# A slot of its own for the diagonal that spreads the maxima, and a generator step between PE products and VectorE's reads

## Chip, cores and metric

The kernel runs on one core of a Trainium2 chip. The metric is the device time of one execution in microseconds (us). A core has five engines that matter here, each with its own instruction queue: PE (TensorE, the matrix products), DVE (VectorE), ACT (ScalarE), POOL (GpSimd) and SP (SyncE, which here issues the DMAs). An engine works its queue in the order of the program and stands still while the instruction at its head waits for another engine or a DMA.

## What is computed

Three stages, each fed by the one before. The reference, cut to what matters:

```python
# 1: attention over a window of 128 positions, 4 x 8 heads of 64, 576 positions
x = attention(q, k, v)                    # 2304 x 512
# 2: soft mixture: 8 experts of 4 slots each
logits = x @ phi
d = softmax(logits, over tokens); slots = d.T @ x
slot_out[e] = relu(slots[e] @ w1[e]) @ w2[e]
x = softmax(logits, over slots) @ slot_out
# 3: mixture over all tokens, gated by Sinkhorn
P = exp(x @ w_gate - max)
for _ in range(8):
    P /= P.sum(1) + 1e-9;  P /= P.sum(0) + 1e-9;  P *= N / E
out = sum over e of P[:, e] * (relu(x @ m1[e]) @ m2[e])
```

The third stage takes most of the time: eight experts of 512 x 1024 and 1024 x 512 weights over 2304 tokens. Here these weights are called `m1` and `m2`.

## The kernel before

The third stage runs a loop over 72 pairs of token tiles, nine pairs for each expert `e`. A pair `m` has seven steps `k_` = 0 to 6. Each product in L1045 is a block of twelve fp16 matmuls (a high and a low half of either factor); the seven products of a pair are those of Strassen's scheme in Winograd's form. Ahead of them, in the first two steps, `emit_z` (L973) makes the hidden values of the next pair in PSUM tiles `z`. From `z`, `left(m+1, k_)` makes the operands `ops` and the sums `s` of the next pair: ACT the high halves and relus, DVE the sums (L998) and some low halves (L986), POOL the other low halves (L1005). The products accumulate in PSUM tiles `x` and `y`; DVE adds them into `acc` (L1057 for expert 0, L1059 for the others) between the products of one `x` tile, so a product that goes on in `x` has to wait until the add in front of it has read the tile.

Beside this loop runs a generator `side`. The call `next(side, None)` in L1194 takes it one step further in each of the 63 steps of an expert, and each `yield` in it ends such a step. What a step issues stands, on every engine, behind the products of that step and ahead of its `left`. In step 4 of an expert's last pair the rest is flushed (L1200). `side` prepares the next expert:

- `prep_w1(e)`: sixteen fp32 products of `st` and `m1` on PE (L682, 32 instructions, since an fp32 matmul is issued twice), the largest magnitude of each row on DVE (`am`, L686), then `spread` (L553): the identity times that column gives a diagonal `dg`; `largest` (L557) multiplies it by a matrix of ones, so that every partition gets all the maxima; DVE takes their maximum (`ar`, L696), makes a power of two of it (L90 to L92), and ACT and DVE write the scaled high and low halves `sh` and `sl` (L701, L702). Two steps later sixteen DMAs copy these to `stk` (L710), eight from each.
- `magnitude(e)`: eight steps of absolute sums of `m2` on ACT (L565), then a maximum (L569).
- `prep_w2a(e)`: `spread` and `largest` again for the maxima of `m2`, then the scaled and differenced halves of `m2` on ACT and POOL in 44 steps.

For expert 0 the first pairs also hold `gate` (products of `st4` with the gate's weights, L904 and L911, a maximum L916, `spread`, `largest`, an exponential into `prob`) beside `magnitude(1)`, and then the eight Sinkhorn rounds (L929 to L942, on DVE with one product on PE, L936) beside `prep_w1(1)` and `prep_w2a(1)`; `par` takes one step of each in turn, and the Sinkhorn side rests in every third.

The diagonal `dg` and the half `sl` are tiles of the pool `mp` with the same tag `sl` and one buffer: each takes its place only when the readers of the one before are done.

Of the kernel before, what the change touches and what calls it, by code (L numbers as in the profile page):

```python
# [8 lines left out]
F32 = mybir.dt.float32  # L9
# [15 lines left out]
def tile_kernel(ctx: ExitStack, tc: tile.TileContext, q, k, v, phi, w1, w2, w_gate, m1, m2, rel, out):  # L25
# [40 lines left out]
    def w1_at(nm, e, dc, f0, n):  # L66
        return wt[nm, e][:, dc * F + f0:dc * F + f0 + n]
# [10 lines left out]
    def warm(pool, tag, w_, n):  # L78

        ps = pool.tile([128, 512], F32, tag=tag, name="warm") if pool is not None else tag  # L80
        for _ in range(n):
            x_ = w_[:, 0:min(256, w_.shape[1])]
            nc.tensor.matmul(ps[:, 0:x_.shape[1]], lhsT=idn, rhs=x_, start=True, stop=True)
        return ps

    def pow2(pool, am, name):

        pw = pool.tile([128, 1], F32, tag=name + "p", name=name + "p")
        iv = pool.tile([128, 1], F32, tag=name + "i", name=name + "i")
        nc.vector.tensor_scalar_max(pw, am, TINY)  # L90
        nc.vector.tensor_single_scalar(pw.bitcast(I32), pw.bitcast(I32), 0x7F800000, op=ALU.bitwise_and)  # L91
        nc.vector.reciprocal(iv, pw)  # L92
        return pw, iv

    with tc.manual_schedule():
        with ExitStack() as ab:
# [5 lines left out]
            with ExitStack() as at:  # L102
# [4 lines left out]
                sp = at.enter_context(tc.tile_pool(name="sp", bufs=2))  # L107
# [426 lines left out]
            mp = ab.enter_context(tc.tile_pool(name="mp", bufs=2, reuse_waits="tile", side="right"))  # L534
# [11 lines left out]
            w2c = {}  # L546
            wsum = {}
            bound = {}

            def spread(am):  # L550

                dg = mp.tile([128, 128], F32, tag="sl", name="dg", bufs=1)
                nc.vector.tensor_scalar_mul(dg, idn, am)  # L553
                return dg

            def largest(dg, ps):
                nc.tensor.matmul(ps, lhsT=ones, rhs=dg, start=True, stop=True)  # L557
# [14 lines left out]
            def prep_w2a(e, place):  # L572
                if e not in bound:
                    yield from magnitude(e)
                dg = spread(bound.pop(e))
                yield
                ps = place()
# [100 lines left out]
            def prep_w1(e, pool=None, tag=None):  # L678
                ps = pool.tile([128, 512], F32, tag=tag, name="m") if pool is not None else pmt
                for dc in range(DC):  # L680
                    for kk in range(4):
                        nc.tensor.matmul(ps[32 * kk:32 * kk + 32, 0:256], lhsT=st[:, dc, :],  # L682
                                         rhs=w1_at("m1", e, dc, 256 * kk, 256),
                                         start=(dc == 0), stop=(dc == DC - 1), tile_position=(0, 32 * kk))
                am = mp.tile([128, 1], F32, tag="am1", name="am1")
                nc.vector.tensor_reduce(out=am, in_=ps[:, 0:256], axis=AX.X, op=ALU.max, apply_absolute_value=True)  # L686
                dg = spread(am)
                if e:
                    yield
                largest(dg, ps[:, 256:384])  # L690
                if e == 0:
                    warm(pool, tag, wt["m1", e], 2)
                else:
                    yield
                ar = mp.tile([128, 1], F32, tag="ar1", name="ar1")
                nc.vector.tensor_reduce(out=ar, in_=ps[:, 256:384], axis=AX.X, op=ALU.max)  # L696
                pw, iv = pow2(mp, ar, "w1")
                nc.vector.tensor_copy(out=inv_s[:, e:e + 1], in_=pw)
                sh = mp.tile([128, 256], F16, tag="sh", name="sh", bufs=1)
                sl = mp.tile([128, 256], F16, tag="sl", name="sl", bufs=1)  # L700
                nc.scalar.activation(out=sh, in_=ps[:, 0:256], func=AF.Copy, scale=iv)  # L701
                nc.vector.scalar_tensor_tensor(out=sl, in0=ps[:, 0:256], scalar=iv, in1=sh,  # L702
                                               op0=ALU.mult, op1=ALU.subtract)
                yield
                yield
                stk[e] = mp.tile([128, F], F16, tag="stk", name="stk")
                if e:
                    for i, part in enumerate((sh, sh, sl, sl)):
                        for kk in range(4):
                            nc.sync.dma_start(out=stk[e][32 * i:32 * i + 32, 256 * kk:256 * kk + 256],  # L710
                                              in_=part[32 * kk:32 * kk + 32, :])
                    yield
                    return
                pss = [pool.tile([128, 512], F32, tag=tag, name="m") for _ in range(4)]
                for lhs, rhs in ((selh, sh), (sell, sl)):
                    for kk in range(4):
                        rows = slice(32 * kk, 32 * kk + 32)
                        nc.tensor.matmul(pss[kk][:, 0:256], lhsT=lhs[rows], rhs=rhs[rows], start=lhs is selh,
                                         stop=lhs is sell, tile_position=(32 * kk, 0))
                for kk in range(4):  # L720
                    (nc.vector.tensor_copy if kk % 2 else nc.scalar.copy)(
                        out=stk[e][:, 256 * kk:256 * kk + 256], in_=pss[kk][:, 0:256])
                yield

            with ExitStack() as bs:
# [154 lines left out]
                for _ in prep_w1(0, pb, "b"):  # L880
                    pass
# [3 lines left out]
            with ExitStack() as ms:  # L885
                ap_ = ms.enter_context(tc.tile_pool(name="acc", bufs=1, reuse_waits="tile"))
                acc = ap_.tile([128, NT, DM], F32, name="acc")

                pmt = pm.tile([128, 512], F32, name="m")
                sp = ms.enter_context(tc.tile_pool(name="sums", bufs=1, reuse_waits="tile"))  # L890
                pz = ms.enter_context(tc.tile_pool(name="pz", bufs=2, reuse_waits="tile", space=PSUM))
                px = ms.enter_context(tc.tile_pool(name="px", bufs=2, reuse_waits="tile", space=PSUM))
                py = ms.enter_context(tc.tile_pool(name="py", bufs=1, reuse_waits="tile", space=PSUM))
# [1 line left out]
                def gate():  # L895

                    st4 = sp.tile([128, DC, 4, NS], F32, name="st4")
                    sgb = sp.tile([128, 4, E], F32, name="sgb")
                    nc.gpsimd.memset(sgb, 0.0)
                    nc.vector.tensor_copy(out=st4, in_=st.unsqueeze(2).to_broadcast([128, DC, 4, NS]))  # L900
                    yield
                    ps = pmt
                    for dc in range(DC):
                        nc.tensor.matmul(ps[:, 0:E], lhsT=st4[:, dc].rearrange("p a b -> p (a b)"),  # L904
                                         rhs=wg_sb[:, dc, :], start=(dc == 0), stop=(dc == DC - 1))
                    for i in range(4):
                        nc.scalar.copy(out=sgb[32 * i:32 * i + 32, i, :], in_=ps[32 * i:32 * i + 32, 0:E])
                    yield
                    yield
                    for g in range(NG):  # L910
                        nc.tensor.matmul(ps[:, 32 * g:32 * g + 32], lhsT=cTf[:, g, :],  # L911
                                         rhs=sgb.rearrange("p a b -> p (a b)"), start=True, stop=True)
                    l2 = ps[:, 0:NT * E]
                    mx = mp.tile([128, 1], F32, tag="mx", name="mx")
                    mg = mp.tile([128, 1], F32, tag="mg", name="mg")
                    nc.vector.tensor_reduce(out=mx, in_=l2, axis=AX.X, op=ALU.max)  # L916
                    dg = spread(mx)
                    yield
                    largest(dg, ps[:, 256:384])
                    yield  # L920
                    nc.vector.tensor_reduce(out=mg, in_=ps[:, 256:384], axis=AX.X, op=ALU.max, negate=True)
                    nc.scalar.activation(out=prob.rearrange("p a b -> p (a b)"), in_=l2, func=AF.Exp, bias=mg)
                    yield
# [237 lines left out]
                for m in range(NM):  # L1161
                    e, n = divmod(m, NP)
# [77 lines left out]
```

## Time and profile before

| | us |
|---|---|
| median of 3 runs | 984.17 (983.91 to 984.69) |
| profiled execution | 984.86 |
| its span on the core | 983.1 |
| PE busy in the span | 950.5 |
| DVE busy | 744.9 |
| ACT busy | 624.4 |
| POOL busy | 574.3 |

The loop over the pairs begins 211 us into the span; attention and the second stage lie before it. An expert takes some 93.5 us. Times in the rows are counted from the start of the span. In the timeline a row is one instruction or some alike, with its start, its length, engine, line, operation, tiles and shapes; a bracket at the end tells how long the engine stood idle before it and which instruction or DMA ended that.

### The profile page before, as it was taken

The numbers are of one execution on the slowest core, as the hardware profiler recorded it, in microseconds if no ns is written. First come the engines' busy times: TensorE is split into PE (matmuls) and PEld (weight loads), VectorE is DVE, ScalarE is ACT, GpSimd is POOL, SyncE is SP. The second block draws the span as 40 slices with busy tenths as digits, with TensorE's granted clock in tenths as the row PEclk, the third lists the DMA queues.
The fourth block names the chain that finished last, engine by engine and source line by source line (L and its number), as shares of the span: only waits on it lengthen the run. The fifth ranks groups of instructions, "written<-read, shape, count | busy, mean of one in ns | idle before, by whom it ended". The sixth has DMA issues, their size and how long they took to land.

```text
span 983.1 us, 24146 instructions
## 1 busy us (share of the span) xinstructions
PE 950.5 (97%) x9341; PEld 814.4 (83%) x9341; DVE 744.9 (76%) x1924; ACT 624.4 (64%) x1529; POOL 574.3 (58%) x685
## 2 busy tenths in 40 slices
PE   8999999889799999999999999999999999999997
PEld 7887886447588888888888888888888888888886
DVE  6988896675697687777777777877777777777775
ACT  5877884746467678766666665766476656664542
POOL 2222210204488568947884797499658956995442
PEclk9999999999899999999999999999999999999999
DMA  8999997970200220031005001300220020001222
GB/s 174 257 226 219 254 281 284 368 267 2 96 1 2 94 90 1 2 109 76 1 2 182 2 1 54 131 2 2 89 95 2 1 94 5 2 2 28 60 44 65
DMA packets 94497, 90.07 MB, mean 92 GB/s; under 512 B 63664, under 2 KB 67632, under 8 KB 94384
## 3 DMA queue, kind: packets, MB, share of 16 engines
q1 hardware_dynamic: 94384, 88.54, 30.9%
q8 instruction: 73, 1.20, 0.5%
q14 instruction: 40, 0.33, 0.1%
HBM read 81.97 MB, written 4.72 MB: 88 GB/s over the span
## 4 chain that ended last, share of the span: by engine, by line
PE 67%; DVE 2%; ACT 0%; issue 0%
PE x L1045 34%; PE y L1045 26%; PE z L973 6%; PE m L682 1%; DVE acc L1059 1%; DVE ops L986 0%; DVE sl L702 0%; ACT sh L701 0%; PE m L557 0%; DVE ar L696 0%; DVE w1i L92 0%; DVE w1p L91 0%; DVE w1p L90 0%; DVE acc L1057 0%; PE m L936 0%
## 5 line engine op out<-in xcount | busy, mean ns | idle before, releaser
L1045 PEld LDWEIGHTS <-ops 128*128 128x128 f16 x6048 | 593.4, 98 | 77.2 <-issue 5.5
L1005 POOL TENSOR_TENSOR ops<-s,ops 128x512 f16<-128x512 f32 x287 | 331.9, 1159 | 234.4 <-ACT ops L1002 196.6
L1045 PE MATMUL x<-w2h,ops 128*128 128x256 f16 x2304 | 415.5, 273 | 4.0 <-DVE acc L1059 3.1
L1045 PE MATMUL y<-w2h,ops 128*128 128x256 f16 x1728 | 319.5, 273 | 0.3 <-POOL ops L1005 0.2
L1002 ACT CAST ops<-s 128x512 f16<-128x512 f32 x288 | 177.8, 618 | 218.5 <-DVE s L998 216.0
L1045 PE MATMUL x<-w2l,ops 128*128 128x256 f16 x1152 | 314.8, 274 | 0.0
L1045 PE MATMUL y<-w2l,ops 128*128 128x256 f16 x864 | 235.6, 273 | 0.0
L1059 DVE SCALAR_TENSOR_TENSOR acc<-x,pe,acc 128x256 f32<-128x256 f32 x252 | 121.8, 483 | 71.1 <-PE x L1045 70.0
L983 ACT ACTIVATE ops<-z 128x512 f16<-128x512 f32 x216 | 128.6, 596 | 36.9 <-PE z L973 34.0
L986 DVE SCALAR_TENSOR_TENSOR ops<-z,ops 128x512 f16<-128x512 f32 x216 | 147.0, 681 | 0.0
L1059 DVE SCALAR_TENSOR_TENSOR acc<-y,pe,acc 128x256 f32<-128x256 f32 x189 | 91.4, 484 | 61.4 <-PE y L1045 60.5
L640 POOL TENSOR_TENSOR w2l<-w,w2h 128x256 f16<-128x256 f32 x168 | 112.9, 676 | 0.0
L998 DVE SCALAR_TENSOR_TENSOR s<-z,r 128x512 f32<-128x512 f32 x144 | 98.2, 682 | 10.3 <-ACT r L994 7.1
L998 DVE SCALAR_TENSOR_TENSOR s<-z,s 128x512 f32<-128x512 f32 x144 | 98.1, 681 | 1.4 <-POOL t L640 0.7
L181 POOL TENSOR_SCALAR qn<-qn 128x128 f32<-128x128 f32 x64 | 33.8, 536 | 100.5 <-DMA qn<-in_q_dram 70.7
L973 PE MATMUL z<-ct,stk 128*128 128x256 f16 x576 | 86.8, 274 | 3.2 <-DVE ops L986 2.5
L643 ACT CAST w2h<-w 128x256 f16<-128x256 f32 x168 | 67.0, 402 | 2.3 <-POOL w L640 2.3
L973 PEld LDWEIGHTS <-stk 128*128 128x128 f16 x576 | 55.6, 98 | 13.1 <-DVE ops L986 3.3
L230 ACT ACTIVATE et<-et,mx 128x192 f32<-128x192 f32 (+2 forms) x144 | 61.3, 434 | 1.2 <-DVE mx L221 1.1
L202 PE MATMUL s<-kT,qT 128*128 128x192 f32 (+2 forms) x288 | 50.2, 317 | 0.1
L221 DVE CUSTOM_DVE_ANT_0 et<-s,rel_sb 128x192 f32<-128x192 f32 (+2 forms) x144 | 40.1, 326 | 8.5 <-PE s L202 8.0
L202 PEld LDWEIGHTS s<-kT,qT 128*128 128x128 f32 x288 | 43.7, 191 | 3.4 <-issue 3.4
(196 smaller groups left out, 949.6 us busy)
## 6 DMA issues: line engine op xcount, KB each, us to landing
w<-in_moe_w_dram SPq DMA_DIRECT2D x68, 512.0 KB, 6.4
w<-in_moe_w_dram SPq DMA_DIRECT2D x14, 2048.0 KB, 8.3
kn<-in_k_dram SPq DMA_DIRECT2D x36, 128.0 KB, 5.4
qn<-in_q_dram SPq DMA_DIRECT2D x36, 128.0 KB, 4.9
v<-in_v_dram SPq DMA_DIRECT2D x18, 256.0 KB, 5.1
out_dram<-acc SPq DMA_DIRECT2D x34, 128.0 KB, 2.4
w<-in_moe_w_dram SPq DMA_DIRECT2D x2, 1024.0 KB, 8.4
stk<-sh SPq DMA_DIRECT2D x56, 16.0 KB, 1.8
```

Source lines behind the costliest of these rows:

```text
L202: nc.tensor.matmul(ps[gg][:, j, col:192], lhsT=qT[:, g, j, :], rhs=kT[:, g, j, k0:k1], start=True, stop=True)
L230: nc.scalar.activation(out=runs[hh], in_=runs[hh], func=AF.Exp, bias=mx[:, hh:hh + 1], scale=-1.0, accum_out=sm[:, hh:hh + 1])
L640: nc.gpsimd.tensor_tensor(out=out_, in0=x_, in1=y_, op=ALU.subtract)
L643: nc.scalar.copy(out=hi[:, i, r], in_=src[:, r])
L973: nc.tensor.matmul(ps[:, i], lhsT=stk[e][:, 128 * ft:128 * ft + 128], rhs=ct.rearrange("p (a n) t -> p a n t", a=2)[:, :, n, :], start=Tru ...
L983: nc.scalar.activation(out=ops_[m][:, k_, 0], in_=zb(m, i, j), func=AF.Relu)
L986: nc.vector.scalar_tensor_tensor(out=ops_[m][:, k_, 1], in0=zb(m, i, j), scalar=0.0, in1=ops_[m][:, k_, 0], op0=ALU.max, op1=ALU.subtract)
L998: nc.vector.scalar_tensor_tensor(out=new_sum(m, nm), in0=zb(m, i, j), scalar=0.0, in1=o, op0=ALU.max, op1=op)
L1002: nc.scalar.copy(out=ops_[m][:, k_, 0], in_=sm_[m, nm])
L1005: eng.tensor_tensor(out=ops_[m][:, k_, 1], in0=sm_[m, nm], in1=ops_[m][:, k_, 0], op=ALU.subtract)
L1045: nc.tensor.matmul(out_, lhsT=a_[:, k_, l_, i, :], rhs=r_[:, k_, i, :], start=(first and j == 0), stop=(j == 11), skip_group_check=True)
L1059: nc.vector.scalar_tensor_tensor(out=o, in0=ps, scalar=pe_[e][:, t:t + 1], in1=o, op0=ALU.mult, op1=ALU.add)
```

## The change

`spread` takes its tile from a pool and tag in `dgp`. At first that is the old slot; when the third stage begins, it becomes a tag `dg` of its own in the pool `sums`, which is opened some lines earlier than before. A `yield` is put between the sixteen products of `prep_w1` and the reduce that reads them (for experts 1 and on), and one between the last products of `gate` and its reduce.

```diff
--- before.py
+++ after.py
@@ -546,10 +546,12 @@
             w2c = {}
             wsum = {}
             bound = {}
+            dgp = [mp, "sl"]
 
             def spread(am):
 
-                dg = mp.tile([128, 128], F32, tag="sl", name="dg", bufs=1)
+                pool, tag = dgp
+                dg = pool.tile([128, 128], F32, tag=tag, name="dg", bufs=1)
                 nc.vector.tensor_scalar_mul(dg, idn, am)
                 return dg
 
@@ -683,6 +685,8 @@
                                          rhs=w1_at("m1", e, dc, 256 * kk, 256),
                                          start=(dc == 0), stop=(dc == DC - 1), tile_position=(0, 32 * kk))
                 am = mp.tile([128, 1], F32, tag="am1", name="am1")
+                if e:
+                    yield
                 nc.vector.tensor_reduce(out=am, in_=ps[:, 0:256], axis=AX.X, op=ALU.max, apply_absolute_value=True)
                 dg = spread(am)
                 if e:
@@ -885,9 +889,10 @@
             with ExitStack() as ms:
                 ap_ = ms.enter_context(tc.tile_pool(name="acc", bufs=1, reuse_waits="tile"))
                 acc = ap_.tile([128, NT, DM], F32, name="acc")
+                sp = ms.enter_context(tc.tile_pool(name="sums", bufs=1, reuse_waits="tile"))
+                dgp[:] = [sp, "dg"]
 
                 pmt = pm.tile([128, 512], F32, name="m")
-                sp = ms.enter_context(tc.tile_pool(name="sums", bufs=1, reuse_waits="tile"))
                 pz = ms.enter_context(tc.tile_pool(name="pz", bufs=2, reuse_waits="tile", space=PSUM))
                 px = ms.enter_context(tc.tile_pool(name="px", bufs=2, reuse_waits="tile", space=PSUM))
                 py = ms.enter_context(tc.tile_pool(name="py", bufs=1, reuse_waits="tile", space=PSUM))
@@ -910,6 +915,7 @@
                     for g in range(NG):
                         nc.tensor.matmul(ps[:, 32 * g:32 * g + 32], lhsT=cTf[:, g, :],
                                          rhs=sgb.rearrange("p a b -> p (a b)"), start=True, stop=True)
+                    yield
                     l2 = ps[:, 0:NT * E]
                     mx = mp.tile([128, 1], F32, tag="mx", name="mx")
                     mg = mp.tile([128, 1], F32, tag="mg", name="mg")
```

The lines after the edits are numbered some higher in the changed kernel: L553 is L555 there, L557 is L559, L686 is L690, L696 is L700, L702 is L706, L929 to L942 are L935 to L948, L986 is L992, L998 is L1004, L1057 is L1063 and L1059 is L1065.

The first place is on DVE, in the Sinkhorn rounds: the end of the row half of a round and what follows, with the waits of each instruction. `am_3647` are the maxima of expert 1's `m2`; In the waits DMAHW stands for DMAs, the other names are engines. Before:

```order
L932 TENSOR_TENSOR prob<-prob,rs 128x144 [waits DVE_49]
L934 TENSOR_REDUCE c_3963<-prob 128x8 [waits DVE_49]
L553 TENSOR_SCALAR dg<-idn,am_3647 128x128 [waits DMAHW4_49,DMAHW5_49,DMAHW3_49,DMAHW6_49,DMAHW2_49,DMAHW7_49,DMAHW1_49,DMAHW0_49]
L998 SCALAR_TENSOR_TENSOR s_4007<-z,r_3983 128x512 [waits PE_49,Activation_49,Pool_49]
L1057 TENSOR_TENSOR acc<-y,acc 128x256 [waits PE_49]
L986 SCALAR_TENSOR_TENSOR ops<-z,ops 128x512
L939 TENSOR_SCALAR c_4042<-m 128x8 [waits PE_49]
L941 RECIPROCAL c_4042<-c_4042 128x8 [waits DVE_49]
L942 TENSOR_TENSOR prob<-prob,c_4042 128x144 [waits DVE_49]
```

and now:

```order
L938 TENSOR_TENSOR prob<-prob,rs 128x144 [waits DVE_49]
L940 TENSOR_REDUCE c_3963<-prob 128x8 [waits DVE_49]
L1004 SCALAR_TENSOR_TENSOR s_4003<-z,r_3966 128x512 [waits PE_49,Activation_49,Pool_49]
L1063 TENSOR_TENSOR acc<-y,acc 128x256 [waits PE_49]
L555 TENSOR_SCALAR dg<-idn,am_3647 128x128
L992 SCALAR_TENSOR_TENSOR ops<-z,ops 128x512
L945 TENSOR_SCALAR c_4041<-m 128x8 [waits PE_49]
L947 RECIPROCAL c_4041<-c_4041 128x8 [waits DVE_49]
L948 TENSOR_TENSOR prob<-prob,c_4041 128x144 [waits DVE_49]
```

The diagonal has moved behind a sum and an add, and it has no wait for DMAs any more; the reduce `ar` that reads the result has moved behind a second sum and add.

The second place is on DVE too, in the first pair of expert 2, where the weights `m1` of expert 3 are prepared. Before, from the reduce `am` on:

```order
L686 TENSOR_REDUCE am_6405<-m 128x1
L553 TENSOR_SCALAR dg<-idn,am_6405 128x128
L1059 SCALAR_TENSOR_TENSOR acc<-x,pe,acc 128x256
L998 SCALAR_TENSOR_TENSOR s_6431<-z,r_6410 128x512
L1059 SCALAR_TENSOR_TENSOR acc<-y,pe,acc 128x256
L696 TENSOR_REDUCE ar_6447<-m 128x1
L90 TENSOR_SCALAR w1p<-ar_6447 128x1
L91 TENSOR_SCALAR w1p<-w1p 128x1
L92 RECIPROCAL w1i<-w1p 128x1
L698 COPY inv_s<-w1p 128x1
L702 SCALAR_TENSOR_TENSOR sl<-m,w1i,sh 128x256
L986 SCALAR_TENSOR_TENSOR ops<-z,ops 128x512
```

and now the same stretch, one add earlier:

```order
L1065 SCALAR_TENSOR_TENSOR acc<-x,pe,acc 128x256
L690 TENSOR_REDUCE am_6405<-m 128x1
L555 TENSOR_SCALAR dg<-idn,am_6405 128x128
L1004 SCALAR_TENSOR_TENSOR s_6430<-z,r_6407 128x512
L1065 SCALAR_TENSOR_TENSOR acc<-y,pe,acc 128x256
L992 SCALAR_TENSOR_TENSOR ops<-z,ops 128x512
L1065 SCALAR_TENSOR_TENSOR acc<-x,pe,acc 128x256
L700 TENSOR_REDUCE ar_6464<-m 128x1
L90 TENSOR_SCALAR w1p<-ar_6464 128x1
L91 TENSOR_SCALAR w1p<-w1p 128x1
L92 RECIPROCAL w1i<-w1p 128x1
L702 COPY inv_s<-w1p 128x1
```

The add of `x` has moved ahead of the reduce, and the low half `ops` and the next add of `x` have moved ahead of the chain from `ar` to `sl`. On PE the matmul L557 stands one block of products later than before, at this place and at each like it; the order of the DMAs on SP is unchanged.

## Rows read from the trace of the kernel before

**Rows 1.** Page, part 1: busy time of the engines, share of the span, instructions.

```profile
PE 950.5 (97%) x9341; PEld 814.4 (83%) x9341; DVE 744.9 (76%) x1924; ACT 624.4 (64%) x1529; POOL 574.3 (58%) x685
```

**Rows 2.** Stretches: length, busy PE, PEld, DVE, ACT, POOL; granted clock, DMA share, GB/s.

```profile
400.00:480.00 80.00, 79.48 (x743) 70.22 (x741) 61.06 (x124) 52.59 (x111) 58.11 (x67) 1.00 0.16 57
```

**Rows 3.** Waits of the whole span: us in total, times, the longest.

```profile
DVE am L686 <- PE m L682: 18.9, 8, 2.6
...
DVE dg L553 <- DMA stk<-sl: 7.0, 1, 7.0
...
PE x L1045 <- DVE acc L1059: 3.1, 6, 0.5
...
PE z L973 <- DVE ops L986: 2.5, 2, 1.6
```

**Rows 4.** Timeline around the diagonal of expert 1's second weights.

```profile
248.57 0.41 DVE L934 TENSOR_REDUCE c<-prob 128x8 f32<-128x144 f32 x1
...
249.73 4.97 SPq L710 DMA_DIRECT2D stk<-sl  x8
...
250.02 0.29 PE L936 MATMUL m<-c,ones 128*128 128x8 f32 x2
...
255.94 0.29 DVE L553 TENSOR_SCALAR dg<-idn,am 128x128 f32<-128x128 f32 x1 [6.96 <-DMA stk<-sl]
...
256.28 0.80 PE L557 MATMUL m<-dg,ones 128*128 128x128 f32 x2 [5.97 <-DVE dg L553]
...
257.20 0.37 PE L1045 MATMUL y<-w2h,ops 128*128 128x256 f16 x1
...
259.72 0.36 PE L1045 MATMUL x<-w2h,ops 128*128 128x256 f16 x1
```

**Rows 5.** Timeline of the first pair of expert 2: PE, DVE, POOL.

```profile
423.54 1.93 PE L682 MATMUL m<-w,st 128*32 128x256 f32 x32
...
425.55 0.42 DVE L686 TENSOR_REDUCE am<-m 128x1 f32<-128x256 f32 x1 [2.56 <-PE m L682]
...
427.17 0.39 PE L557 MATMUL m<-dg,ones 128*128 128x128 f32 x2
...
427.37 0.48 DVE L1059 SCALAR_TENSOR_TENSOR acc<-y,pe,acc 128x256 f32<-128x256 f32 x1
427.39 0.27 PE L1045 MATMUL x<-w2h,ops 128*128 128x256 f16 x1
...
427.77 0.28 DVE L696 TENSOR_REDUCE ar<-m 128x1 f32<-128x128 f32 x1
...
428.70 0.27 PE L1045 MATMUL y<-w2h,ops 128*128 128x256 f16 x1
...
429.57 0.68 DVE L986 SCALAR_TENSOR_TENSOR ops<-z,ops 128x512 f16<-128x512 f32 x1
...
430.17 0.47 DVE L1059 SCALAR_TENSOR_TENSOR acc<-x,pe,acc 128x256 f32<-128x256 f32 x1
...
430.69 0.27 PE L1045 MATMUL x<-w2h,ops 128*128 128x256 f16 x1 [0.52 <-DVE acc L1059]
...
432.02 2.28 POOL L1005 TENSOR_TENSOR ops<-s,ops 128x512 f16<-128x512 f32 x2 [1.15 <-ACT ops L1002]
...
435.28 0.38 PE L1045 MATMUL x<-w2h,ops 128*128 128x256 f16 x2
...
436.37 0.60 PE L973 MATMUL z<-ct,stk 128*128 128x256 f16 x4
```

**Rows 6.** Stretches as in rows 2; then one line's instructions: ns min/median/max, first and last start.

```profile
257.20:259.70 2.50, 2.50 (x12) 1.72 (x12) 2.33 (x10) 1.03 (x3) 1.16 (x1) 0.50 1.01 354
256.00:288.00 32.00, 30.91 (x263) 26.29 (x264) 30.48 (x72) 20.60 (x48) 23.39 (x27) 0.94 0.18 66
...
L932 DVE TENSOR_TENSOR prob<-prob,rs x8: 307/485/966, 237.4 to 297.2; 128x144 f32<-128x144 f32 x8
```

**Rows 7.** Timeline at the end of the Sinkhorn rounds, PE.

```profile
299.68 0.50 PE L973 MATMUL z<-ct,stk 128*128 128x256 f16 x3 [1.65 <-DVE ops L986]
```

## The prediction

> **Bound.** The page was read first. TensorE (PE) is busy 950.5 of 983.1 us [rows 1]. A busy PE need not be at its peak, so the stages were read next: in a steady stretch of 80 us PE is busy 79.48 and VectorE (DVE) only 61.06 [rows 2]. There the products of L1045 follow each other without a break, and a change can win only what PE still waits for. The third view, the waits, names four things that touch the edited lines [rows 3]: DVE's diagonal `dg` waits once, 7.0 us, for the DMAs that read `sl`; DVE's reduce `am` waits eight times for the sixteen products of `prep_w1`, 18.9 us in all; PE waits for DVE's adds before `x` products six times, 3.1 us; PE waits twice for DVE's `ops` before `z`, 2.5 us. The last view, the timeline, says which of these waits reach PE: the first [rows 4] and the third [rows 5]. DVE works strictly in program order, so whatever is queued behind a waiting instruction waits too.
>
> **Part 1** is the slot of its own. Before, `dg` and the half-weights `sl` share one buffer. For expert 1 the diagonal of `prep_w2a` comes right after the DMAs are issued (the magnitudes were taken earlier, beside the gate), so it must wait until all eight transfers out of `sl` have landed. DVE ends its work at 248.98 and starts `dg` at 255.94: 6.96 us. PE has `largest` next in its queue and stands still 5.97 us [rows 4]. Behind the waiting `dg`, DVE holds the sums `s`, the add and the `ops` of the next pair, and ScalarE and GpSimd wait for those in turn. In the changed order the same `dg` carries no DMA wait, as the listing in front shows. For experts 2 to 7 nine steps of `magnitude` lie between the DMAs and `dg`, and `dg` waits for nothing there (the wait stands once in the row), so the slot costs and gains nothing. The diagonal's multiply itself is unchanged; a 512-byte tile per partition is added and no instruction.
>
> What is this wait worth? Two bounds. PE: with `dg` ready, `L936` at 250.02 would be followed by `largest` and then by the `y` products; such an fp32 product takes PE about 0.22 us (L1045 resumed 0.22 us after `largest` started at 427.17 [rows 5]), so `y` would start at 250.46 and the next `x` 1.31 us later, at 251.77. It started at 259.72, so PE lost 7.95 us [rows 4, 5]. DVE: 6.96 us. Between the two I take DVE's, because DVE is last in this stage: from 256 to 288 it is busy 30.48 of 32.00 us, since the Sinkhorn rounds lie on it beside the products' own work [rows 6], and the stage ends with PE waiting 1.65 us for DVE's `ops` at 299.68 [rows 7]. A DVE that starts 6.96 us earlier and has the same work ends 6.96 us earlier. So part 1 gives 7.0 us, ends 6.0 (PE's idle row alone) and 8.0.
>
> The clock speaks to that choice. The twelve `y` products after the stall took 2.52 us instead of 1.31; the granted clock in that stretch was 0.50, the 1.2 GHz level, and PE had stood idle 5.97 us before [rows 4, 6]. The Trainium skill (TensorE: Matmul & The Clock Gate, section HAM oscillation) says that an idle gap throttles the array and that the next matmuls pay for it; by this rule PE gets the slow stretch back too and part 1 is worth 7.95 us. That is PE's bound above, and it counts in full only where DVE keeps up.
>
> **Part 2** is the step between the products and the reduce in `prep_w1`. Once per expert from 2 to 7 (six times; the rows show the preparation of expert 3) PE gets sixteen fp32 products at 423.54, 1.93 us long. DVE is free at 422.99 and stands before the reduce until 425.55, 2.56 us, with the add of `x` behind it [rows 5]. It never catches up before the next add of `x`: that runs at 430.17, and the `x` product needs it. PE's `y` started at 428.70, its twelve take 1.31 us (427.39 to 428.70), so the next product was due at 430.01; it came at 430.69. The loss is 0.68 us (the row's 0.52 counts from the modelled end of the last matmul) [rows 5].
>
> Now the new order, with the starts of these rows (an add takes DVE 0.40 us from start to start, an `ops` or `s` 0.60, the chain from `ar` to `sl` 1.80, that is 427.77 to 429.57). The add of `x` goes in front of the reduce: it needs the `x` products that end just before 423.54 plus their drain, so it runs at 423.65. The reduce then still waits until 425.55; the wait doesn't vanish, only what is behind it shrinks. `s` follows the reduce and the diagonal; the `y` add runs at 427.37 as before, `ops` at 427.77, and the critical add of `x` as soon as its products end, about 428.68 instead of 430.17. PE needs it at about 430.0, `largest` being a step later, so the 0.68 us is gone. What is late next: the chain now lies behind that add, 429.08 to 430.88, and then come `s`, add, `s`, add, `ops`, add, `s`, add, `ops`: 430.88 + 5 x 0.60 + 4 x 0.40 = 435.5. The last `ops` frees the PSUM buffer of the second `z`, which came at 436.37 and without the stall is due at 435.69 [rows 5]. So it just fits, with 0.2 us to spare. The gain is 6 x 0.68 = 4.1 us, ends 0 and 4.1.
>
> **Part 3** is the step in the gate, and what shifts behind both steps. The gate's reduce moves behind one sum and one add. PE does not wait for it: the matrix `prob` is first read by Sinkhorn only after the ten rounds of `magnitude`, so I cost it at nothing; that cover is the magnitudes' ten rounds against the gate's seven, now eight. The reduce of expert 1's preparation (one of the eight in [rows 3]) also sheds a sum and an add from behind it, 0.60 + 0.40 us, but the chain to `sl` then waits for a later `largest`; I take 0, with ends 0 and 0.4, an estimate: the 1.0 us less the 0.60 of one more instruction's wait. Every later step of the preparation moves by one, and so do its DMAs: SyncE's queue keeps its order, and `stk` is needed only by the next expert, tens of us later. At the end of an expert what is left over is flushed at once: one more copy on ScalarE and one more subtract on GpSimd than before. Their results are used seven products later; nothing.
>
> Sum: 7.0 + 4.1 = 11.1 us. The profiled execution took 984.86 us, of which 983.1 is the span; it would take 973.8. The median of the runs shown is 984.17, 0.69 lower, so 973.1 is forecast.
>
> **Rivals.**
> 1. *DVE is late at `z`.* The chain of 1.80 us behind the critical add lands on the second `z`, where I count only 0.2 us to spare; if `sl` waits for ScalarE longer, part 2 gives nothing. Then 984.17 - 7.0 - 0.4, about 976.8. For: the margin is thin. Against: DVE idles again in a steady stretch (61.06 of 80.00).
> 2. *PE keeps all of it.* DVE, freed at the gate, at the reduce and at `dg`, gets far enough ahead that PE's `z` waits vanish as well: 7.95 + 2.5 [rows 3] + 4.1 = 14.6, so 969.6. For: DVE's waits before 250 also shrink. Against: 30.48 of 32.00.
> 3. *The saved time is lost to GpSimd.* The multiply of a Sinkhorn round takes 0.307 us at best, 0.485 in the middle and 0.966 at worst [rows 6], the longer ones while GpSimd is busy with weights (23.39 of 32 us). If the twelve multiplies of the last six rounds all went from the middle to the worst, that is 12 x 0.48 = 5.8 us, of which about half is already paid: 3 us, giving 976. The Trainium skill (SBUF - State Buffer, section Who interferes with whom) speaks for it: a VectorE instruction with two SBUF inputs contends with a GpSimd instruction that reads SBUF, and the change pushes both together. Against: the rounds that ran beside an idle GpSimd before 249 do so still.
> 4. *Slower.* The weights' subtracts on GpSimd shift by one step against the products' low halves (L1005). The tightest of those, for the second sum, ends at 433.18 (the first of the two at 432.02, 1.16 each) and PE reads it at 435.28 [rows 5]: 2.1 us of slack. A subtract takes 0.68, so from four in front of it PE would wait; at 0.68 in each of the some 44 pairs with a preparation that is 30 us, 1003. Against: one step of the preparation issues one subtract.
> 5. *It doesn't do what it says*: the slot still waits, on whatever lay in that memory. 984. Against: the order shows no wait at all.
>
> **Chances.** Forecast 0.57, rival 1 0.14, rival 2 0.15, rival 3 0.07, rival 4 0.03, rival 5 0.04. The forecast's own range is 971.7 to 974.5. With rivals 1, 2 and 3 the range is 969.4 to 977.2; rivals 4 and 5 and the tails stay out. Faster by over 0.2% (2 us, about what a measurement here tells from no change): 0.93; within: 0.04; slower: 0.03.
>
> **What shows it.** In the changed trace `dg` has no DMA releaser, PE's 5.97 us is gone and the clock holds at 1.00 from 250 to 260; the gaps of PE for `z` in the Sinkhorn stage stay (rival 2 if they go). The six waits for the add of `x` are gone and no wait of `z` stands in their place (rival 1 if one does); the period from one expert's sixteen products to the next falls by 0.68 us; DVE's reduce still waits some 1.5 us each. I would be wrong if the Sinkhorn stage gave back the start, or if the first pair of each expert got a new gap.

## The result, and the profile after

The changed kernel takes **975.25 us** (median of four runs, 974.01 to 977.06), the kernel before 984.04 us (four runs, 983.87 to 984.69) on the same chip. The ratio is 0.9911, with a 95% interval of 0.9894 to 0.9928: faster by 8.8 us, where 11.1 were forecast. The profiled execution of the changed kernel took 975.7 us, of which 973.9 is the span. Of the lines named below, L682 is now L684, L710 is L714, L973 is L979, L1005 is L1011 and L1045 is L1051; in the experiments the numbers differ from those of the changed kernel by the one to three lines that each edit leaves out or adds.

Page, part 1, after (engine, busy us, share of the span, instructions; answers to [rows 1]):

```profile
PE 947.7 (97%) x9341; PEld 813.8 (84%) x9341; DVE 744.7 (76%) x1924; ACT 624.8 (64%) x1529; POOL 575.3 (59%) x685
```

The instructions are the same. Of the 9.2 us by which the span shrank, 6.4 are idle time of PE and 2.8 busy time. The waits, after (engine, line, what it waited for: us in total, times, the longest; answers to [rows 3]):

```profile
DVE am L690 <- PE m L684: 10.1, 7, 1.7
...
PE z L979 <- DVE ops L992: 3.8, 2, 2.2
...
DVE am L690 <- PE m L942: 1.8, 1, 1.8
```

Two rows of before have no counterpart: the wait of `dg` for the DMAs out of `sl` (7.0 us) and the six waits of the `x` products for DVE's add (3.1 us). The reduce's waits are shorter, as forecast, and still there. But one of them has a releaser that it did not have before, Sinkhorn's product L942, and the waits at `z` have grown from 2.5 to 3.8 us.

The steady stretch answers to [rows 2] (length, busy PE, PEld, DVE, ACT, POOL; granted clock, DMA share, GB/s): PE now has no gap in it at all.

```profile
400.00:480.00 80.00, 80.00 (x749) 70.83 (x747) 62.26 (x127) 51.96 (x111) 58.09 (x67) 1.00 0.17 57
```

The diagonal of expert 1's second weights, in the timeline of after (answers to [rows 4]; start us, us, engine, line, operation, and in brackets the idle time ahead and its releaser): it runs with no DMA releaser, in front of the transfers that it used to wait for.

```profile
251.55 0.65 DVE L555 TENSOR_SCALAR dg<-idn,am 128x128 f32<-128x128 f32 x1
251.85 4.96 SPq L714 DMA_DIRECT2D stk<-sl  x8
```

Two marks divide the span so that each part of the change can be read alone: the first `z` of expert 0 (at 211.63 before, 211.37 after) and the last waiting `z` of the Sinkhorn rounds ([rows 7] before; 294.61 after, below). From the one to the other runs expert 0's stage with the gate, Sinkhorn and expert 1's preparation; behind the second lie the rest of expert 0 and experts 1 to 7, with the preparations of experts 2 to 7.

| | first `z` to last waiting `z` | from there to the span's end |
|---|---|---|
| before | 299.68 - 211.63 = 88.05 | 983.1 - 299.68 = 683.42 |
| after | 294.61 - 211.37 = 83.24 | 973.9 - 294.61 = 679.29 |

The tail gave 4.13 us, what part 2 was said to give. The stage gave 4.81 us instead of 7.0. So the question is where 2.2 us of the stage went. The timeline of after around expert 1's preparation shows a candidate:

```profile
237.31 1.93 PE L684 MATMUL m<-w,st 128*32 128x256 f32 x32
...
240.50 0.29 PE L942 MATMUL m<-c,ones 128*128 128x8 f32 x2
240.82 0.42 DVE L690 TENSOR_REDUCE am<-m 128x1 f32<-128x256 f32 x1 [1.80 <-PE m L942]
...
242.90 1.16 POOL L1011 TENSOR_TENSOR ops<-s,ops 128x512 f16<-128x512 f32 x1 [2.32 <-ACT ops L1008]
243.11 1.11 DVE L948 TENSOR_TENSOR prob<-prob,c 128x144 f32<-128x144 f32 x1
...
244.15 0.28 DVE L700 TENSOR_REDUCE ar<-m 128x1 f32<-128x128 f32 x1
...
246.87 0.68 DVE L992 SCALAR_TENSOR_TENSOR ops<-z,ops 128x512 f16<-128x512 f32 x1
...
247.61 1.03 PE L979 MATMUL z<-ct,stk 128*128 128x256 f16 x4 [2.22 <-DVE ops L992]
...
294.61 0.61 PE L979 MATMUL z<-ct,stk 128*128 128x256 f16 x4 [1.56 <-DVE ops L992]
```

The sixteen products end at 239.24, but the reduce begins only at 240.82. One step later in the order, it stands behind Sinkhorn's first product, which writes other columns of the same PSUM tile `pmt` (384 on, where the reduce reads 0 to 255), and the program has it wait for that too. (The Trainium skill, PSUM — Partial Sum Buffer, section PSUM bank collisions raise a hardware error, asks for waits by bank and quadrant, not by address; by this rule the wait is needed as long as both lie in one bank. The trace agrees in so far as a wait stands at disjoint columns; no run leaves it out, and none gives Sinkhorn's sums a tile of their own.) Behind the reduce the chain `ar` to `sl` comes late, and with it the `ops` that frees the buffer of `z`. PE stands still 2.22 us, where the same `z` waited 0.81 before:

```profile
246.95 0.61 PE L973 MATMUL z<-ct,stk 128*128 128x256 f16 x4 [0.81 <-DVE ops L986]
```

And the twelve `y` products behind that gap take 2.56 us (248.43 to 250.99) instead of 1.31, at a granted clock of 0.50, the 1.2 GHz level:

```profile
248.40:251.00 2.60, 2.60 (x15) 1.82 (x13) 1.72 (x5) 1.46 (x4) 0.15 (x2) 0.50 0.09 19
```

### The profile page after: what moved, and what is told of

It is laid out like the page before. It is cut to its first block, busy times and chain, and to the rows that moved or that the text cites. A ratio compares the mean times of both kernels' runs of the same rounds, so it can differ in the third digit from the quotient of the medians.

```text
span 973.9 us, 24118 instructions
## 1 busy us (share of the span) xinstructions
PE 947.7 (97%) x9341; PEld 813.8 (84%) x9341; DVE 744.7 (76%) x1924; ACT 624.8 (64%) x1529; POOL 575.3 (59%) x685
## 4 chain that ended last, share of the span: by engine, by line
PE 69%; DVE 0%; issue 0%
PE x L1051 35%; PE y L1051 27%; PE z L979 6%; PE m L684 1%; PE m L559 0%; DVE ops L992 0%; DVE acc L1065 0%; DVE acc L1063 0%; PE m L942 0%
## 5 line engine op out<-in xcount | busy, mean ns | idle before, releaser
L1051 PEld LDWEIGHTS <-ops 128*128 128x128 f16 x6048 | 592.9, 98 | 72.8 <-issue 1.8
L1011 POOL TENSOR_TENSOR ops<-s,ops 128x512 f16<-128x512 f32 x287 | 332.7, 1161 | 228.2 <-ACT ops L1008 227.3
L1051 PE MATMUL x<-w2h,ops 128*128 128x256 f16 x2304 | 414.3, 273 | 1.8 <-ACT ops L989 0.7
L1051 PE MATMUL y<-w2h,ops 128*128 128x256 f16 x1728 | 319.5, 273 | 0.0
L1051 PE MATMUL x<-w2l,ops 128*128 128x256 f16 x1152 | 314.2, 273 | 0.0
L1051 PE MATMUL y<-w2l,ops 128*128 128x256 f16 x864 | 235.6, 273 | 0.0
L1065 DVE SCALAR_TENSOR_TENSOR acc<-x,pe,acc 128x256 f32<-128x256 f32 x252 | 121.7, 483 | 77.4 <-PE x L1051 76.1
L992 DVE SCALAR_TENSOR_TENSOR ops<-z,ops 128x512 f16<-128x512 f32 x216 | 146.9, 680 | 0.0
L1065 DVE SCALAR_TENSOR_TENSOR acc<-y,pe,acc 128x256 f32<-128x256 f32 x189 | 91.3, 483 | 58.4 <-PE y L1051 58.1
L1004 DVE SCALAR_TENSOR_TENSOR s<-z,r 128x512 f32<-128x512 f32 x144 | 98.2, 682 | 11.2 <-ACT r L1000 7.2
L1004 DVE SCALAR_TENSOR_TENSOR s<-z,s 128x512 f32<-128x512 f32 x144 | 98.1, 682 | 5.0 <-ACT ops L989 4.8
L979 PE MATMUL z<-ct,stk 128*128 128x256 f16 x576 | 86.8, 274 | 4.5 <-DVE ops L992 3.8
L979 PEld LDWEIGHTS <-stk 128*128 128x128 f16 x576 | 55.6, 98 | 14.4 <-DVE ops L992 4.8
```

What stands on the lines that cost most here:

```text
L979: nc.tensor.matmul(ps[:, i], lhsT=stk[e][:, 128 * ft:128 * ft + 128], rhs=ct.rearrange("p (a n) t -> p a n t", a=2)[:, :, n, :], start=Tru ...
L992: nc.vector.scalar_tensor_tensor(out=ops_[m][:, k_, 1], in0=zb(m, i, j), scalar=0.0, in1=ops_[m][:, k_, 0], op0=ALU.max, op1=ALU.subtract)
L1004: nc.vector.scalar_tensor_tensor(out=new_sum(m, nm), in0=zb(m, i, j), scalar=0.0, in1=o, op0=ALU.max, op1=op)
L1011: eng.tensor_tensor(out=ops_[m][:, k_, 1], in0=sm_[m, nm], in1=ops_[m][:, k_, 0], op=ALU.subtract)
L1051: nc.tensor.matmul(out_, lhsT=a_[:, k_, l_, i, :], rhs=r_[:, k_, i, :], start=(first and j == 0), stop=(j == 11), skip_group_check=True)
L1065: nc.vector.scalar_tensor_tensor(out=o, in0=ps, scalar=pe_[e][:, t:t + 1], in1=o, op0=ALU.mult, op1=ALU.add)
```

## The experiments

Theory A, then: the slot is worth its 7 us, the step is worth 4.1 us in experts 2 to 7, and for expert 1 the step costs some 2 us, because the reduce then also waits for Sinkhorn's product. Rivals: the slot itself is worth only 4.8 (B); the gate's step is what costs (C); the step is late by itself, whatever Sinkhorn does (D).

**The parts apart.** `slot_only` has neither step:

```diff
-                if e:
-                    yield
                 nc.vector.tensor_reduce(out=am, in_=ps[:, 0:256], ...
...
-                    yield
                     l2 = ps[:, 0:NT * E]
```

> Only the slot of its own; neither the gate nor the preparation gives a step. Theory A (the slot is worth the forecast 7 us; the preparation's step costs about 2 us for expert 1, where the reduce of the maxima then also waits for Sinkhorn's product that writes the same PSUM tile, and it gives 6 x 0.69 = 4.1 us for experts 2 to 7): 984.0 - 7.2 = 976.8 us; the wait of the product z at 247.61 us after is short again (0.8 us before) and the reduce of expert 1 begins within 1 us of its products' end. Theory B (the step costs nothing for expert 1, and the slot itself is worth only the 4.8 us that the stage lost, the rest being given back in Sinkhorn's chain): 984.0 - 4.8 = 979.2 us, with a wait of about 2 us at the same z.

Measured: 977.22 us against 984.46 for the kernel before in the same rounds, 7.24 us faster (in brackets, here and below, the ratio to before with its 95% interval: 0.9922, 0.9909 to 0.9935). The same stretch of its timeline, and the last waiting `z`:

```profile
237.46 1.93 PE L684 MATMUL m<-w,st 128*32 128x256 f32 x32
239.46 0.42 DVE L688 TENSOR_REDUCE am<-m 128x1 f32<-128x256 f32 x1 [1.79 <-PE m L684]
...
241.66 0.28 DVE L698 TENSOR_REDUCE ar<-m 128x1 f32<-128x128 f32 x1
...
246.43 0.61 PE L976 MATMUL z<-ct,stk 128*128 128x256 f16 x4 [0.80 <-DVE ops L989]
...
292.09 0.61 PE L976 MATMUL z<-ct,stk 128*128 128x256 f16 x4 [1.64 <-DVE ops L989]
```

The reduce begins right behind its products, `z` waits 0.80 us, and the stage takes 80.67 us, 7.38 less than before; of these, 7.07 lie between this `z` and the last waiting one (45.66 us instead of 52.73), where the diagonal stands. The tail is 683.31, as before. Theory B falls.

`slot_from2` has the slot, and the preparation's step from expert 2 on:

```diff
-                if e:
+                if e > 1:
                     yield
...
-                    yield
                     l2 = ps[:, 0:NT * E]
```

> The slot of its own, and the preparation's step for experts 2 to 7 alone; none in the gate. Theory A: both gains without the cost of expert 1's step, 984.0 - 7.2 - 4.1 = 972.7 us, faster than the changed kernel by some 2 us. Theory B: the same as the changed kernel, 984.0 - 4.8 - 4.1 = 975.1 us.

Measured: 973.21 us (0.9884, 0.9868 to 0.9899), 4.01 us less than `slot_only`, on the same chip; the tail of its trace is 972.9 - 293.64 = 679.26, as in the changed kernel. So the gain of the six steps is whole, and the kernel without expert 1's step is the faster one.

`slot_nogate` is the changed kernel without the gate's step:

```diff
-                    yield
                     l2 = ps[:, 0:NT * E]
```

> The changed kernel without the gate's step: slot of its own, and the preparation's step for experts 1 to 7. Theory A (expert 1's step costs the 2 us): as the changed kernel, 975.2 us, with the wait of 2.2 us at z. Theory C (the gate's step, by which Sinkhorn's first rounds stand otherwise, is what costs): about 973 us, with that wait gone.

Measured: 974.91 us (0.9897, 0.9883 to 0.9911): 1.70 us more than `slot_from2`, from which it differs by expert 1's step alone, and level with the changed kernel. Its `z` waits as there:

```profile
246.87 0.88 PE L978 MATMUL z<-ct,stk 128*128 128x256 f16 x4 [2.21 <-DVE ops L991]
```

`steps_only` leaves the diagonal in its old slot:

```diff
-                dgp[:] = [sp, "dg"]
```

> The steps in the gate and in the preparation, with the diagonal in its old slot. Theory A: 4.1 us gained in experts 2 to 7, up to 2 us lost in expert 1, and the wait of TensorE behind the diagonal of expert 1 (5.97 us before) is still there: 980 to 982 us. Theory B: 4.1 us gained and nothing lost, 979.9 us. If the two parts of the change only work together, it is nearer to 984.

Measured: 982.30 us (0.998, 0.9971 to 0.9989), 2.2 us faster than before, just outside theory A's range (by 0.3) and far from theory B's 979.9. If the six steps gave their 4.1, expert 1's step cost 1.9. The trace shows only a part of this: its tail is 4.1 us shorter than before, and from the sixteen products to the last waiting `z` it takes 62.76 us where before took 61.70, so 1.06 lost. (It was taken in the quickest of the eleven runs, 980.75 us; what the others lost beyond it stays open.) The wait for the DMAs is back, and so is a long gap of PE:

```profile
247.21 0.61 PE L978 MATMUL z<-ct,stk 128*128 128x256 f16 x4 [2.21 <-DVE ops L991]
...
257.04 0.29 DVE L555 TENSOR_SCALAR dg<-idn,am 128x128 f32<-128x128 f32 x1 [6.83 <-DMA stk<-sl]
...
258.06 0.49 PE L559 MATMUL m<-dg,ones 128*128 128x128 f32 x2 [4.50 <-DVE c L944]
```

**The gate's step, beside the changed kernel again.** `after_again` is the changed kernel unaltered.

> The changed kernel once more, on the chip and in the rounds of the three others of this call, so that they have it to stand against: 975.25 us, within 0.7 us.

Measured: 975.30 us, against 984.99 for before (0.9894, 0.9879 to 0.9909). `gate_from2` is `slot_from2` with the gate's step put back, that is, the changed kernel without expert 1's step:

```diff
-                if e:
+                if e > 1:
                     yield
```

> Slot, preparation's step from expert 2 on, and the gate's step. Forecast of the prediction (the gate's step is worth 0 to 0.4 us) and theory A: 972.8 to 973.2 us, against 973.2 without it. Theory C (the gate's step is dear together with the rest): 973.5 us or more, up to 975.

Measured: 973.04 us (0.9875, 0.986 to 0.989): 2.26 us less than `after_again`, and 0.17 less than `slot_from2` (from another set of rounds, in which the kernel before took 0.53 us less). So the gate's step costs nothing that the runs can tell, and theory C falls. Its last waiting `z` stands at 292.02 and its first `z` at 211.48: the stage takes 80.54 us, against 294.91 - 211.77 = 83.14 in `after_again`, 2.60 more. From the start of the sixteen products to the waiting `z` it is 10.30 us in `after_again` and 8.98 in `gate_from2`; from that `z` to the last waiting one it is 47.04 and 45.69. So 1.32 us are lost up to the `z`, and 1.35 behind it, where the clock is at half for a while.

**Is it Sinkhorn's product?** So far the runs show that expert 1's step costs 2 us, not why. `swap` keeps the step and puts the preparation ahead of Sinkhorn in every round of that side work, so that the reduce no longer stands behind the product:

```diff
-                    live, i = [x_, y_], 0
+                    live, i = ([y_, x_] if rests else [x_, y_]), 0
```

> The changed kernel with the preparation ahead of Sinkhorn in each round of expert 0's side work, so that the reduce of expert 1's maxima stands ahead of Sinkhorn's first product in the same PSUM tile; the step for expert 1 stays. Theory A (the step is dear because the reduce, one step later, then also waits for that product, and Sinkhorn's three operations stand ahead of the chain to the scales): the reduce begins at its products' end, the wait at z is 0.8 us or less, the granted clock stays 1.00 from 245 to 255 us, and the time is that of the kernel with the slot and the steps from expert 2 on, 973.2 us, or up to 0.7 us less. Theory D (the step itself, with the work that stands ahead of the reduce, makes the chain late, whatever Sinkhorn does): 975.2 us with a wait of about 2 us at z.

Measured: 975.01 us (0.9893, 0.9878 to 0.9908). By the time alone this is theory D. The timeline and the stretches say otherwise:

```profile
239.28 0.42 DVE L690 TENSOR_REDUCE am<-m 128x1 f32<-128x256 f32 x1 [0.29 <-PE m L684]
...
246.47 0.61 PE L979 MATMUL z<-ct,stk 128*128 128x256 f16 x4 [1.11 <-DVE ops L992]
...
251.42 0.17 DVE L945 TENSOR_SCALAR c<-m 128x8 f32<-128x8 f32 x1 [1.20 <-PE m L559]
...
257.20 0.39 PE L942 MATMUL m<-c,ones 128*128 128x8 f32 x2 [1.90 <-DVE c L940]
```

```profile
245.00:255.00 10.00, 8.89 (x83) 7.78 (x81) 8.46 (x26) 4.68 (x10) 3.48 (x3) 1.00 0.11 27
255.00:265.00 10.00, 8.11 (x59) 6.33 (x58) 7.88 (x19) 6.93 (x16) 6.96 (x8) 0.83 0.59 213
```

The reduce waits 0.29 us instead of 1.80, `z` 1.11 instead of 2.22, and the clock holds at 1.00 there: what theory A said of this place came true, but for the 0.8 us or less that it had for `z`. But the swap turned the same coin over in a later round. Now Sinkhorn's read of its sums (`c`, L945) stands behind the preparation's product in the same tile and waits 1.20 us for it; the next Sinkhorn product comes 1.90 us late, and the clock falls behind that gap (0.83 over 255 to 265). One loss was traded for its like: up to the `z` it is 9.19 us now instead of 10.30, but from there to the last waiting `z` 47.72, where `gate_from2` takes 45.69. `swap_first` therefore swaps in the first two rounds alone:

```diff
-                        for g_ in list(live):
+                        for g_ in (live[::-1] if rests and i < 2 else list(live)):
```

> The changed kernel with the preparation ahead of Sinkhorn in the first two rounds of expert 0's side work alone, so that the reduce of expert 1's maxima and its diagonal stand ahead of Sinkhorn's first product; from the third round on the order is the changed kernel's, so that the swap's late product of Sinkhorn (a wait of TensorE of 1.90 us, with the clock at half behind it) is not to be expected. Theory A (expert 1's step is dear because its reduce then waits for Sinkhorn's product too, which makes the scales and the product z behind them late and lets the clock fall): the wait at z falls from 2.2 to about 1.1 us as in the swap, the granted clock is 1.00 from 245 to 265 us, and the time is 973.0 us, within 0.6 us. Theory D (the step itself makes the chain late): 975.2 us, with a wait at z of about 2 us and a fallen clock.

Measured: 973.33 us (0.989, 0.9872 to 0.9908), level with the kernels that lack expert 1's step, with the step still in. It ran in rounds of its own: against the kernel before in them (984.55) it gains 11.2 us, `after_again` in its rounds 9.7, and the intervals of the two ratios overlap. The trace is sharper. The timeline, and the stretches:

```profile
238.60 0.42 DVE L690 TENSOR_REDUCE am<-m 128x1 f32<-128x256 f32 x1 [0.51 <-PE m L684]
...
241.06 1.16 POOL L1011 TENSOR_TENSOR ops<-s,ops 128x512 f16<-128x512 f32 x1 [1.41 <-ACT ops L1008]
...
242.10 0.31 DVE L948 TENSOR_TENSOR prob<-prob,c 128x144 f32<-128x144 f32 x1
242.32 0.28 DVE L700 TENSOR_REDUCE ar<-m 128x1 f32<-128x128 f32 x1
...
245.79 0.61 PE L979 MATMUL z<-ct,stk 128*128 128x256 f16 x4 [1.12 <-DVE ops L992]
```

```profile
245.00:255.00 10.00, 8.83 (x80) 7.73 (x80) 9.59 (x27) 6.21 (x13) 4.78 (x5) 1.00 0.10 26
255.00:265.00 10.00, 9.49 (x87) 8.34 (x88) 9.40 (x23) 6.43 (x16) 6.29 (x8) 1.00 0.60 214
```

This is the closest comparison of all. The code is written in another order, but reduce and product are on different engines, so that DVE's row of instructions in this stage is the same as in the changed kernel, one by one, and so is GpSimd's: only the reduce's wait is for an earlier product. Two stretches in the middle of the stage tell the kernels apart:

| | sixteen products to the waiting `z` | from there to the last waiting `z` |
|---|---|---|
| before | 8.97 | 52.73 |
| `slot_only` (no step) | 8.97 | 45.66 |
| `gate_from2` (no step for expert 1) | 8.98 | 45.69 |
| `after_again` (the changed kernel) | 10.30 | 47.04 |
| `swap_first` (the step, the reduce ahead) | 9.19 | 45.77 |

With that wait alone gone, 2.4 of the 2.7 us are back. Theory A is shown as to the cause; theory D keeps 0.2 us, the step's own share.

The way from the wait to `z` is not only the wait, though. Counted from the end of the sixteen products, Sinkhorn's multiply L948 begins after 3.57 us in `swap_first` and after 3.87 in the changed kernel, 0.30 later; the reduce `ar` behind it comes after 3.79 and 4.91, 1.12 later. The other 0.8 us is the multiply itself, which runs 1.11 us beside a subtract of GpSimd (L1011, at 242.90) that the same delay has pushed onto it, and 0.31 us where the subtract is nearly over. It takes 1.11 in all four kernels that have expert 1's step in the old order, and 0.31 in the seven others. That the subtract is what lengthens it fits these rows; no run moves the subtract alone.

**A second step.** `two_steps` asks whether more of the same helps in experts 2 to 7, where the reduce of `slot_from2` still waits 1.41 us:

```diff
                 if e > 1:
                     yield
+                    yield
```

> Slot, and two steps in place of one between products and reduce for experts 2 to 7; no step for expert 1 and none in the gate. Theory E (one step takes all that there was, since TensorE has no wait left behind it in these experts): 973.2 us, within 0.5 us. Theory F (the vector engine's remaining wait of about 1.7 us at the reduce still costs; the second step covers it): 6 x 0.3 to 0.7 us less, 969 to 971.4 us. Theory G (a second step makes the scales late for the z products that use them): slower than 974 us, with new waits of TensorE at z in experts 2 to 7.

Measured: 975.24 us (0.9893, 0.9876 to 0.991), 2.2 us slower than `gate_from2` beside it and 2.0 slower than `slot_from2`. The six waits of the reduce are gone, but DVE has not lost its waiting: it now stands 2.64 us before the add of `y` ahead of the reduce. And the time is longer. The second `z` behind the preparation, in `two_steps` and then in `slot_from2`, and the sixteen products of two experts running:

```profile
509.82 1.93 PE L684 MATMUL m<-w,st 128*32 128x256 f32 x32
...
513.64 0.48 DVE L1065 SCALAR_TENSOR_TENSOR acc<-y,pe,acc 128x256 f32<-128x256 f32 x1 [2.64 <-PE y L1051]
514.04 0.41 DVE L691 TENSOR_REDUCE am<-m 128x1 f32<-128x256 f32 x1
...
520.22 0.60 PE L979 MATMUL z<-ct,stk 128*128 128x256 f16 x4
...
522.18 0.61 PE L979 MATMUL z<-ct,stk 128*128 128x256 f16 x4
...
602.86 1.93 PE L684 MATMUL m<-w,st 128*32 128x256 f32 x32
```

```profile
509.63 1.93 PE L684 MATMUL m<-w,st 128*32 128x256 f32 x32
...
511.63 0.42 DVE L690 TENSOR_REDUCE am<-m 128x1 f32<-128x256 f32 x1 [1.41 <-PE m L684]
...
520.02 0.60 PE L978 MATMUL z<-ct,stk 128*128 128x256 f16 x4
...
521.77 0.60 PE L978 MATMUL z<-ct,stk 128*128 128x256 f16 x4
...
602.43 1.93 PE L684 MATMUL m<-w,st 128*32 128x256 f32 x32
```

From one `z` to the next it is 1.96 us instead of 1.75, and from expert to expert 93.04 instead of 92.80: 0.24 us, six times, or 1.4 us (its tail is 1.52 longer; the rest of the 2 us lies in no stretch that the traces tell apart from the spread of the runs). That is theory G, in small: the reduce, 2.2 us later behind its products (4.22 instead of 2.00), makes the chain to `sl` late, and with it the `ops` that free `z`, which end at 522.12 in `two_steps`, 0.06 us before that `z`. It is rival 1 of the prediction, one step further on. PE's own row shows no wait there: the modelled end of the product before it lies at 522.12 as well.

## Why the prediction was nearly right

**The bound and the views.** That a change could win only what PE waits for, and that the timeline says which waits reach PE, held in the main: the span fell by 9.2 us, the busy time of PE by 2.8.

**Part 1, the slot: right.** 7.0 us with ends 6.0 and 8.0; alone it measured 7.24, and its stage shrank by 7.38. The choice between DVE's bound (6.96) and PE's (7.95) fell on the right one: the `z` at the stage's end still waits for DVE, 1.64 us beside 1.65 before. From the waiting `z` ahead of the diagonal to that one it gave 7.07 us, DVE's bound to 0.1; so of the 0.99 us between the two bounds hardly anything came.

**Part 2, the step for experts 2 to 7: right.** 6 x 0.68 forecast; 4.01 us between two kernels, 4.13 in the tail, a period of 92.80 us (510.59 - 417.79) where it was 93.49. The walk through the new order holds row by row. Everything in after stands 5.75 us earlier; with that, the critical add was due at 422.93, the chain's end at 425.13 and the second `z` at 429.94:

```profile
422.92 0.48 DVE L1065 SCALAR_TENSOR_TENSOR acc<-x,pe,acc 128x256 f32<-128x256 f32 x1 [0.23 <-PE x L1051]
...
425.12 0.68 DVE L1004 SCALAR_TENSOR_TENSOR s<-z,s 128x512 f32<-128x512 f32 x1
...
429.93 0.60 PE L979 MATMUL z<-ct,stk 128*128 128x256 f16 x4
```

The margin of 0.2 us at that `z` was real too (the `ops` that frees it ends 0.17 us before it, 429.08 + 0.68 against 429.93): the second step used it up.

**Part 3, "what shifts behind both steps": here the step failed.** The gate's share at nothing was right as far as the runs can tell. The share of expert 1 was put at 0, with ends 0 and 0.4 of gain; it is a loss of 1.7 (`slot_nogate` against `slot_from2`) to 2.3 us (`after_again` against `gate_from2`), and no end of the range for it lay below nothing. For experts 2 to 7 the prediction followed the new order instruction by instruction; for expert 1, where Sinkhorn's products run in the same tile beside the preparation, it counted the sum and the add that were shed and the wait for one later `largest`, but neither the wait of the reduce for Sinkhorn's product nor Sinkhorn's three operations (L945 to L948) that now stand ahead of `ar`. The row that would have said it was there to be asked for: the product of Sinkhorn (L936, at 241.17 in the trace of before) writes `m`, as the preparation's do, and the reduce was one step away from it. For the same reason one sign that was named held only in part: from 250 to 251 us the granted clock was still 0.50, and 1.00 from there to 260.

**The rivals.** Rival 1 did not come with one step, and came with two. Rival 2 fell: the waits at `z` stayed. Rival 3, GpSimd, came in one row instead of twelve: L948, 1.11 us beside 0.31 at best, under a subtract of GpSimd (242.90 to 244.06), which is 0.8 of the 1.1 us by which the reduce's wait made `z` late. It hangs on that wait: in `swap_first`, with the same instructions, it is gone. The rule of the Trainium skill that the prediction cites (SBUF — State Buffer, section Who interferes with whom) agrees with that row: both inputs of the multiply, and the subtract's, lie in SBUF. Rivals 4 and 5 fell.

**The sum by the runs**: 7.24 + 4.01 + 0.17 - 2.26 = 9.16 us, where 8.8 and, in the second comparison, 9.7 were measured (the terms come from two sets of rounds). The forecast of 973.1 us was 2.15 too low, within its range of 969.4 to 977.2; the kernels without the flaw measured 973.0 to 973.3.

**A version better than both** follows: `gate_from2`, with the step from expert 2 on, at 973.04 us, or `swap_first` at 973.33; their difference is less than the spread of their runs.

## What to carry to other kernels

A step put between a product and its reader moves the reader behind everything that is issued in that step; where one of these writes the same PSUM tile, the reader waited for it too here, even at other columns. Follow the new order separately for each place where the step runs, the one with other work beside it first, and give the step only to those places that gain. A wait that vanishes from the profile is no gain in itself: the second step removed six, put them elsewhere, and cost 2 us.

## What the runs showed of the hardware

The price of a wait of PE was not its length. Behind the `z` gap of 2.22 us the granted clock was 0.50 and the next twelve products took 1.25 us more; it fell at this place in all four traces with a gap of 2.2 us there, and in none of the seven with 0.80 to 1.12. Behind Sinkhorn's gap of 1.90 us in `swap` it fell as well (0.50 from 259 to 261 us); behind the 1.64 us at the end of the stage in `slot_only` it stayed:

```profile
285.00:300.00 15.00, 13.36 (x124) 11.76 (x123) 13.00 (x27) 9.86 (x23) 11.94 (x15) 1.00 0.01 2
```

(The Trainium skill, TensorE: Matmul & The Clock Gate, section HAM oscillation, has the matmuls behind an idle gap pay for it; the traces agree that they do behind some gaps, and show that much shorter waits than the 5.97 us of before are among these.) The length of one gap does not settle it: behind the 0.8 us that PE waits in the gate, the same in all eleven traces, the clock fell in six (in before to 0.50 from 226 to 229 us) and stayed in five. What decides is not shown. For the reader this means two things: a `z` that came 1.32 us later cost 2.67 us of the stage, so a change that only lengthens an existing wait can cost twice what the wait row shows; and a stage that begins ahead of such a place is measured with it, so the stretches compared above begin behind it.
